# Three moves in the opening of a retention, feed-forward and expert kernel: weights through a PSUM bank, one scaling on VectorE, one output earlier

## The chip, the cores and the metric

The kernel runs on one core of a Trainium2 chip. The metric is the time of one execution in microseconds, device side; a lower time is better. TensorE is the matrix engine, VectorE (DVE), ScalarE (ACT) and GpSimd (POOL) work on vectors, and SyncE (SP) issues most transfers. Steps and chunks are counted from 0.

## The reference

Three stages in a row: retention (attention with a decay and no softmax), a feed-forward layer whose weights come in as 64-bit floats, and a layer of eight experts with a capacity of 288 tokens each.

```python
scores = scale * np.matmul(q, k.transpose(0, 1, 3, 2))          # B, H, S, D = 4, 8, 576, 64
ret = scores * np.where(rel >= 0, gamma ** rel, 0.0)
x = np.matmul(ret, v)                                            # to 2304 tokens of 512

h = x @ w_in                                                     # 512 -> 2048
g = h * np.tanh(np.log1p(np.exp(h)))
x = g @ w_out                                                    # 2048 -> 512

logits = x @ w_gate                                              # 8 experts
# the largest logits first: each token to one expert, 288 tokens to each expert
out[mask] = np.maximum(x[mask] @ w1[e], 0.0) @ w2[e]
```

## The kernel before

The change lies in `first_part`, which does the retention and the feed-forward layer; the experts follow in `second_part`, which is not touched.

The tokens go in chunks of 128 or 64 for the retention and in blocks of 256 for the feed-forward layer. A chunk has three parts. `a_scores` makes the scores on TensorE (line 223) into two PSUM banks, multiplies both by the decay on VectorE (line 228, tile `pm`), scales q on GpSimd (line 232) and k on GpSimd or VectorE (line 237). `a_out` multiplies with the running state (line 247) and with v (line 252) into a third bank, and splits the result into a high half `xh` on ScalarE (line 258) and a low half `xl` on VectorE (line 259). `a_state` adds to the state (line 277).

The feed-forward layer runs in steps: step i takes one of 16 column tiles of `w_in` and the matching tile of `w_out` for one block. `ff_h` makes `ph`, twelve products from high and low halves (line 323). `ff_a1` turns it on ScalarE into `d` (lines 332 to 334) and multiplies on VectorE (line 340, here called the product), `ff_a2` takes the reciprocal (line 345), `ff_b1` makes `u` (line 350), `ff_b2` finishes it (line 358), and `ff_b3` splits it into `gh` on ScalarE (line 364) and `gl` on VectorE or GpSimd (line 365). `ff_y` multiplies with `w_out` three steps later (line 417).

In the first 35 steps or so each step also converts a weight tile. A weight comes as 64-bit numbers of two 32-bit words. `x1` (line 163) and `c` (line 160) read them on ScalarE, `x` (line 167) and `a` (line 172) put the bits together on VectorE, `h` rounds the high half on ScalarE (line 178), and `l` takes the low half on GpSimd (line 181). Four tiles are begun ahead of step 0, so the tile whose `c` stands at the end of step i is shifted and joined in step i + 1 by

```python
        def a(self):
            t = self.t.bitcast(U32)
            nc.vector.scalar_tensor_tensor(t, t, 3, self.w0, op0=ALU.logical_shift_left,
                                           op1=ALU.bitwise_or)
```

Each engine works through its own queue in the order in which the Python code emits, and waits at the head of it. Parts of chunks 2 to 6 are put into steps by the table `EARLY` (line 30): scores of chunk 2 into step 0, its output and state into step 1, scores of chunk 3 into step 2, its output and state into step 3, scores of chunk 4 into step 4, of chunk 5 into step 5, of chunk 6 into step 7. A step that converts calls these parts behind `ff_a1` and `ff_b3`. The banks A to E go round (`bank`, line 200); from step 3 on A and B hold the output of block 0, and from step 7 on C and D that of block 1. Block 1, with steps 4 and 5, needs the outputs of chunks 2 and 3. `fill` issues products on TensorE that nobody reads (line 506).

Of the kernel before, what the change touches and what calls it, by code (L numbers as in the profile page):

```python
# [7 lines left out]
F32 = mybir.dt.float32  # L8
# [4 lines left out]
U32 = mybir.dt.uint32  # L13
U16 = mybir.dt.uint16
I64 = mybir.dt.int64
AF = mybir.ActivationFunctionType
ALU = mybir.AluOpType

P = 128
B, H, S, D = 4, 8, 576, 64  # L20
N, DM, FF, E, F = 2304, 512, 2048, 8, 1024
# [9 lines left out]
MID = (2, 3, 5, 8, 8, 9, 11, 14)  # L31
JOIN = (9, 14)
YL = 3
NF = FF // P


# [24 lines left out]
LOG2 = (3, 4, 6)  # L61
TAIL = (NB - 1) * NF


def plan():


    spread = lambda a, b, n: [a + (b - a) * k // (n - 1) for k in range(n)]
    own = {i: (0, f) for f, i in enumerate([0, 1, 2, 3] + spread(6, ENDS[0], NF - 4))}
    free = [i for i in range(3 * NF) if i not in own]  # L70
    lead = [i for i in free if i < BEGIN2]
    rest = [i for i in free if BEGIN2 <= i]
    near = [i for i in rest if i <= ENDS[1]]
    ones = lead + [near[k] for k in spread(1, len(near) - 1, NF - len(lead))]
    own.update({i: (1, f) for f, i in enumerate(ones)})
# [6 lines left out]
def first_part(ctx, tc, att, att_ht, att_hn, dtab, qtab, ktab, stab, wi, wo, wgb, ydram, L, constants, cst, begin, grid):  # L82
    nc = tc.nc
# [9 lines left out]
    D_ = big.tile([P, 2, 4, P], F32, name="dt")  # L93
# [19 lines left out]
    def load_chunk(ci):  # L113
        load_qk(ci)
        load_v(ci)
# [27 lines left out]
    class convert:  # L143
# [8 lines left out]
            self.i = done[0]  # L152
            done[0] += 1

        def c(self):
            if self.i in (2, 3):
                self.t = spare[:, self.i % 2 * 512:][:, :512]
            else:
                self.t = cvs[self.i % 2]
            nc.scalar.activation(self.t, self.w1.bitcast(F32), AF.Copy, scale=2.0 ** -112)  # L160

        def x1(self):
            nc.scalar.activation(self.w0, self.top, AF.Copy, scale=2.0 ** -13, bias=-0.4999)
# [1 line left out]
        def x(self):  # L165
            w0 = self.w0
            nc.vector.scalar_tensor_tensor(w0, self.w1, 0x80000000, w0, op0=ALU.bitwise_and,  # L167
                                           op1=ALU.bitwise_or)

        def a(self):  # L170
            t = self.t.bitcast(U32)
            nc.vector.scalar_tensor_tensor(t, t, 3, self.w0, op0=ALU.logical_shift_left,  # L172
                                           op1=ALU.bitwise_or)
            if self.i not in (6, 7):
                fetch()
# [18 lines left out]

    att_tags = ["A", "B", "C", "D", "E"]
    turn = [0]

    def bank(tag=None):  # L200
        if not tag:
            tag = att_tags[turn[0] % len(att_tags)]
            turn[0] += 1
        return psum.tile([P, 4, P], F32, tag=tag, name="b_" + tag)
# [10 lines left out]
    def a_scores(ci, halves=(0, 1), tags=(None, None), eng=nc.gpsimd):  # L215
        b, s0, n = CHUNKS[ci]
        a = at_tiles[ci]
        qT = a[:, 0, 0:4 * n].rearrange("p (h t) -> p h t", h=4)
        kT = a[:, 1, 0:4 * n].rearrange("p (h t) -> p h t", h=4)
        ts = [(s, bank(tags[s])) for s in halves]  # L220
        for hp in range(4):
            for s, t in ts:
                nc.tensor.matmul(t[:n, hp, :n], kT[s * 64:(s + 1) * 64, hp, :],  # L223
                                 qT[s * 64:(s + 1) * 64, hp, :], start=True, stop=True)
        if 0 in halves:
            pm[ci] = work.tile([P, 2, 4, P], F32, tag="pm", name="pm")
        for s, t in ts:
            nc.vector.tensor_mul(pm[ci][:n, s, :, :n], t[:n, :, :n], D_[:n, s, :, :n])
        if 1 not in halves:
            return  # L230
        if s0 > 0:
            nc.gpsimd.tensor_mul(qT, qT, Q_[:, :, :n])
        if s0 + n < S:
            kn = a[:n, 2, :].rearrange("p (h d) -> p h d", h=H)
            s1 = since(ci)
            c = 4 + (s1 + 64) // P if s1 % P or n < P else s1 // P
            eng.tensor_mul(kn, kn, K_[:n, c, :, None].to_broadcast([n, H, D]))
# [56 lines left out]
    def micro(n):  # L294

        out = []
        for ci in chunks_of(n):
            if n == 3:
                out.append([lambda ci=ci: a_scores(ci, (0,))])
                out.append([lambda ci=ci: a_scores(ci, (1,))])  # L300
            else:
                out.append([lambda ci=ci: a_scores(ci)])
            out.append([lambda ci=ci: a_out(ci)])
            out.append([lambda ci=ci: a_state(ci),
                        lambda ci=ci: load_chunk(ci + 2) if ci + 2 < len(CHUNKS) else None])
        return out
# [8 lines left out]
    def ff_h(n, f, i):  # L315
        xh, xl = x_block(n)
        if i % 2 == 0:
            hbank[0] = psum.tile([P, 2, TB], F32, tag=("ph0", "ph1")[i // 2 % 2], name="ph")
        ph = hbank[0][:, i % 2, :]
        k = 0  # L320
        for kt in range(KT):
            for w, x in ((winh, xh), (winl, xh), (winh, xl)):
                nc.tensor.matmul(ph, w[f][:, kt, :], x[:, kt, :], start=(k == 0), stop=(k == 11))  # L323
                k += 1
        q2[n, f] = ph

    def ff_a1(n, f, i, alone):

        ph = q2[n, f]
        d = work.tile([P, 2, P], F32, tag="d", name="d", bufs=2)  # L330
        df = d.rearrange("p a b -> p (a b)")
        nc.scalar.activation(df, ph, AF.Tanh, scale=0.5)  # L332
        nc.scalar.activation(df, df, AF.Square, bias=half_b, scale=-0.5)  # L333
        nc.scalar.activation(df, df, AF.Copy, bias=0.5, scale=0.5)  # L334
        u = work.tile([P, 2, P], F32, tag="u", name="u", bufs=3)
        r = u[:, 0, :]
        if alone:

            r = rs[:, i % 2 * P:][:, :P]
        nc.vector.tensor_mul(r, d[:, 0, :], d[:, 1, :])  # L340
        inv[n, f] = (d, u, r, alone)
# [144 lines left out]
    slots = {}  # L486
# [12 lines left out]
    c0, c1, old, now = [convert() for j in range(4)]  # L499
    for hp in range(WARM):  # L500
        nc.tensor.matmul(state[0][:, hp % 4, :], SD[:, 0, :], SD[:, 0, :], start=True, stop=True)
    unread = psum.tile([P, 2, TB], F32, tag="ph1", name="unread")

    def fill(n):
        for k in range(n):
            nc.tensor.matmul(unread[:, 0, :P], D_[:, 0, 0, :], D_[:, 0, 1, :], start=True, stop=True)

    a_scores(0)
    fill(2)
# [33 lines left out]
    for j, m in zip(MID, micro(3)):  # L543
        slots.setdefault(steps.index((0, NF - 1)) + YL + j, []).extend(m)
    slots.setdefault(3 * NF + 5, []).append(lambda: a_scores(chunks_of(4)[0]))
# [12 lines left out]
    for x in slots.get(-1, []):  # L558
        x()
    for i in range(len(steps) + YL):  # L560
        new = i < len(steps)
        if not i or new and not_yet(i):
            ff_h(*steps[i], i)
        if i == 20:
            constants()
        if i == 62:
            stage.__exit__(None, None, None)
            late = tc.tile_pool(name="late", bufs=1)
            WG = late.__enter__().tile([P, E, DM], F32, name="WG")
            nc.sync.dma_start(WG, wgb)  # L570
        if now:
            now.x()
            now.a()
        if old:
            old.l()
        if new:
            n, f = steps[i]
            alone = bool(now or old)
            eng = nc.vector if alone else nc.gpsimd
            if not alone:  # L580
                for x in slots.get(i, []):
                    x()
            if i and steps[i - 1] in inv:
                ff_b1(*steps[i - 1], nc.vector)
            ff_a1(n, f, i, alone)
            if i > 1:
                ff_b3(*steps[i - 2], eng)
            if alone:
                for x in slots.get(i, []):
                    x()  # L590
            if now:
                now.h()
            if alone or i == len(steps) - 2:
                ff_h(*steps[i + 1], i + 1)
            while behind:
                behind.pop()()
            ff_a2(n, f)
            if i:
                ff_b2(*steps[i - 1])
            if eng is not nc.vector:  # L600
                ff_b1(n, f, nc.vector if i == len(steps) - 1 else eng)
        if i == len(steps) - 1:
            ff_b2(n, f)
            ff_b3(*steps[i - 1], nc.gpsimd)
            ff_b3(n, f, nc.vector)
        old, now = now, None
        if nxt and i in CONV:
            now, nxt = nxt, convert() if done[0] < len(parts) else None
            now.x1()
            now.c()  # L610
        for k in range(2 if i % 4 == 0 or TAIL <= i < POP2 else 1):
            if idle:
                idle.pop(0)()
        if late and i > TAIL + BEGIN and not idle:
            late = late.__exit__(None, None, None)
            soon.extend(begin())
        if i >= YL:
            ff_y(*steps[i - YL], i)
    while idle:
# [1019 lines left out]
```

## Time and profile before

| what | us |
|---|---|
| median of three runs | 793.83 |
| lowest and highest | 793.38, 793.94 |
| the profiled execution | 800.43 |
| its span | 798.6 |
| busy: TensorE | 756.1 |
| busy: VectorE | 541.0 |
| busy: GpSimd | 483.3 |
| busy: ScalarE | 435.2 |

The span is that of one execution taken with the profiler on. It shows the order and the durations of single instructions; changes of the time are read against the median of the runs. The share of a busy engine is an average over stages that have different limits.

### The profile page before, as it was taken

The numbers are of one execution on the slowest core, as the hardware profiler recorded it, in microseconds if no ns is written. First come the engines' busy times: TensorE is split into PE (matmuls) and PEld (weight loads), VectorE is DVE, ScalarE is ACT, GpSimd is POOL, SyncE is SP. The second block draws the span as 40 slices with busy tenths as digits, with TensorE's granted clock in tenths as the row PEclk, the third lists the DMA queues.
The fourth block names the chain that finished last, engine by engine and source line by source line (L and its number), as shares of the span: only waits on it lengthen the run. The fifth ranks groups of instructions, "written<-read, shape, count | busy, mean of one in ns | idle before, by whom it ended". The sixth has DMA issues, their size and how long they took to land.

```text
span 798.6 us, 16299 instructions
## 1 busy us (share of the span) xinstructions
PE 756.1 (95%) x6163; PEld 698.4 (87%) x6163; DVE 541.0 (68%) x1260; ACT 435.2 (54%) x944; POOL 483.3 (61%) x546
## 2 busy tenths in 40 slices
PE   7799899999999999999999999949999999999995
PEld 6687777898989998989889999839899989999995
DVE  5999998555646897997988976666566754542220
ACT  4789997545445545555555564414444644644631
POOL 2643333555546676676675665327688988978921
PEclk9999999999999999999999999958999999999998
DMA  9556442010333200212010000045466567556411
GB/s 344 201 180 217 158 146 75 28 31 24 106 99 114 80 27 27 81 54 80 16 38 27 2 27 2 1 160 189 145 190 189 172 200 221 164 165 218 136 31 32
DMA packets 27380, 87.79 MB, mean 110 GB/s; under 512 B 4464, under 2 KB 5616, under 8 KB 27168
## 3 DMA queue, kind: packets, MB, share of 16 engines
q1 hardware_dynamic: 24160, 77.06, 29.7%
q0 software_dynamic: 3136, 9.64, 3.7%
q8 instruction: 49, 0.80, 0.4%
q14 instruction: 35, 0.29, 0.1%
HBM read 77.25 MB, written 9.44 MB: 109 GB/s over the span
## 4 chain that ended last, share of the span: by engine, by line
PE 72%; DVE 13%; issue 7%; POOL 2%; ACT 2%; DMA 2%; another core or an unknown queue 0%; POOLq 0%; SPq 0%; DVEq 0%; ACTq 0%
PE ph L323 20%; PE hp L1336 10%; PE op L1350 10%; PE b_E L417 8%; PE b_F L417 8%; DVE rs L345 3%; DVE y L172 2%; DVE raw L167 2%; PE cnt L1045 1%; PE b_A L223 1%; DVE u L350 1%; POOL wxl L876 1%; PE b_D L252 1%; PE b_E L453 1%; PE b_F L453 1%
## 5 line engine op out<-in xcount | busy, mean ns | idle before, releaser
L323 PE MATMUL ph<-xh,winh 128*128 128x256 f32 x576 | 164.9, 286 | 8.4 <-ACT d L332 5.4
L323 PE MATMUL ph<-xl,winh 128*128 128x256 f32 x576 | 160.7, 279 | 0.8 <-DVE xl L259 0.8
L323 PE MATMUL ph<-xh,winl 128*128 128x256 f32 x576 | 160.8, 279 | 0.0
L876 POOL TENSOR_TENSOR wxl<-wraw,wxh 128x1024 fp32r<-128x1024 f32 x63 | 149.3, 2394 | 9.0 <-ACT wxh L874 7.5
L323 PEld LDWEIGHTS ph<-xh,winh 128*128 128x128 f32 x576 | 108.5, 188 | 23.8 <-ACT d L332 9.9
L365 POOL TENSOR_TENSOR gl<-u,gh 128x256 fp32r<-128x256 f32 x114 | 88.9, 780 | 62.9 <-ACT gh L364 62.2
L332 ACT ACTIVATE d<-ph 128x256 f32<-128x256 f32 x144 | 54.9, 381 | 128.8 <-PE ph L323 114.5
L323 PEld LDWEIGHTS ph<-xh,winl 128*128 128x128 f32 x576 | 108.6, 189 | 4.0
L345 DVE RECIPROCAL u<-u 128x128 f32<-128x128 f32 x113 | 107.7, 953 | 3.9
L323 PEld LDWEIGHTS ph<-xl,winh 128*128 128x128 f32 x576 | 108.6, 189 | 1.3 <-DVE xl L259 1.3
L340 DVE TENSOR_TENSOR u<-d 128x128 f32<-128x128 f32 x113 | 53.4, 473 | 60.6 <-ACT d L334 60.0
L352 POOL TENSOR_TENSOR u<-d,u 128x128 f32<-128x128 f32 x112 | 51.7, 461 | 58.8 <-DVE u L345 58.8
L333 ACT ACTIVATE d<-d,half_b 128x256 f32<-128x256 f32 x144 | 73.5, 511 | 4.7
L874 ACT ACTIVATE wxh<-wraw 128x1024 fp32r<-128x1024 f32 x64 | 67.3, 1053 | 13.6 <-DMA wraw<-in_wx_dram 13.6
L353 POOL TENSOR_TENSOR u<-d,u 128x128 f32<-128x128 f32 x112 | 68.8, 614 | 8.8
L334 ACT ACTIVATE d<-d 128x256 f32<-128x256 f32 x144 | 60.2, 418 | 4.5
L364 ACT ACTIVATE gh<-u 128x256 fp32r<-128x256 f32 x144 | 58.1, 403 | 5.4 <-DVE u L358 4.4
L374 DVE SCALAR_TENSOR_TENSOR scr<-y,WG 128x512 bf16<-128x512 f32 x64 | 56.4, 881 | 0.4
L1327 DVE SCALAR_TENSOR_TENSOR htl<-hp,hth 128x288 fp32r<-128x288 f32 x64 | 29.1, 455 | 35.1 <-ACT hth L1339 34.2
L358 DVE SCALAR_TENSOR_TENSOR u<-u,ph 128x256 f32<-128x256 f32 x144 | 52.0, 361 | 0.0
L1339 ACT ACTIVATE hth<-hp 128x288 fp32r<-128x288 f32 x64 | 26.1, 409 | 43.4 <-PE hp L1336 34.5
L1336 PE MATMUL hp<-xth,wxh 128*128 128x288 f32 x256 | 49.4, 307 | 0.0
(299 smaller groups left out, 1874.6 us busy)
## 6 DMA issues: line engine op xcount, KB each, us to landing
wraw<-in_wx_dram SPq DMA_DIRECT2D x64, 512.0 KB, 4.4
att<-in_att_dram SPq DMA_DIRECT2D x32, 512.0 KB, 5.8
raw<-in_wi_dram SPq DMA_DIRECT2D x16, 512.0 KB
raw<-in_wo_dram SPq DMA_DIRECT2D x16, 512.0 KB, 3.2
ydram<-y SPq DMA_DIRECT2D x9, 512.0 KB, 2.8
WG<-in_wgb_dram SPq DMA_DIRECT2D x1, 2048.0 KB
att<-in_att_ht_dram SPq DMA_DIRECT2D x4, 256.0 KB
att<-in_att_hn_dram SPq DMA_DIRECT2D x4, 256.0 KB
```

The source lines that it names most:

```text
L323: nc.tensor.matmul(ph, w[f][:, kt, :], x[:, kt, :], start=(k == 0), stop=(k == 11))
L333: nc.scalar.activation(df, df, AF.Square, bias=half_b, scale=-0.5)
L334: nc.scalar.activation(df, df, AF.Copy, bias=0.5, scale=0.5)
L345: nc.vector.reciprocal(r, r)
L353: eng.tensor_mul(u[:, 0, :], d[:, 1, :], r)
L364: nc.scalar.activation(gh, g, AF.Copy)
L365: eng.tensor_sub(gl, g, gh.bitcast(F32))
L417: nc.tensor.matmul(py[n][t], g[:, t * P:(t + 1) * P], w[f], start=(f == 0 and w is woh and g is gh), stop=(f == NF - 1 and g is gl))
L874: nc.scalar.activation(hi, raw, AF.Copy)
L876: rest = lambda eng: eng.tensor_sub(lo, raw, hi.bitcast(F32))
L1336: nc.tensor.matmul(hp, W[ft // 2][w][:, s], x[:, kt, :], start=(k == 0), stop=(k == 11))
L1350: nc.tensor.matmul(op, W[4 + dt][w][:, s], h[:, ft, :], start=(k == 0), stop=(k == 23))
```

## The change

Four edits. The tiles whose `c` stands in steps 0 and 1 leave `c` in PSUM bank E, and `a` reads it there and writes the same SBUF tile as before; so that bank E is free for this, the first chunks go round four banks, and E joins them again at step 4. The k of chunk 3 is scaled on VectorE. In step 3 `ff_a1` and the parts of chunk 3 (output and state, with the loads of chunk 5) come ahead of `u` of step 2 and `gl` of step 1. Six unread products into bank E stand behind them.

```diff
+SOON = 3
...
-        def c(self):
+        def c(self, aside=False):
...
-            nc.scalar.activation(self.t, self.w1.bitcast(F32), AF.Copy, scale=2.0 ** -112)
+            self.s = bank("E").rearrange("p a b -> p (a b)") if aside else self.t
+            nc.scalar.activation(self.s, self.w1.bitcast(F32), AF.Copy, scale=2.0 ** -112)
...
-            t = self.t.bitcast(U32)
-            nc.vector.scalar_tensor_tensor(t, t, 3, self.w0, op0=ALU.logical_shift_left,
+            nc.vector.scalar_tensor_tensor(self.t.bitcast(U32), self.s.bitcast(U32), 3, self.w0, op0=ALU.logical_shift_left,
                                            op1=ALU.bitwise_or)
...
-    att_tags = ["A", "B", "C", "D", "E"]
+    att_tags = ["A", "B", "C", "D"]
...
-                out.append([lambda ci=ci: a_scores(ci)])
+                out.append([lambda ci=ci: a_scores(ci, eng=nc.vector if ci == 3 else nc.gpsimd)])
...
-    def fill(n):
+    def fill(n, to=unread[:, 0, :P]):
         for k in range(n):
-            nc.tensor.matmul(unread[:, 0, :P], D_[:, 0, 0, :], D_[:, 0, 1, :], start=True, stop=True)
+            nc.tensor.matmul(to, D_[:, 0, 0, :], D_[:, 0, 1, :], start=True, stop=True)
...
+        if i == SOON + 1:
+            att_tags.append("E")
...
-            if not alone:
-                for x in slots.get(i, []):
-                    x()
+            todo = list(slots.get(i, []))
+            if i == SOON:
+                ff_a1(n, f, i, alone)
+            if not alone or i == SOON:
+                while todo:
+                    todo.pop(0)()
             if i and steps[i - 1] in inv:
                 ff_b1(*steps[i - 1], nc.vector)
-            ff_a1(n, f, i, alone)
+            if i != SOON:
+                ff_a1(n, f, i, alone)
             if i > 1:
                 ff_b3(*steps[i - 2], eng)
-            if alone:
-                for x in slots.get(i, []):
-                    x()
+            while todo:
+                todo.pop(0)()
+            if i == SOON:
+                fill(6, bank("E")[:, 0, :])
...
-            now.c()
+            now.c(i < 2)
```

VectorE's queue from `a` of step 2 to the end of step 3, before (`y_153` holds the joined weight, `raw` its two words, `rs` the reciprocal):

```order
L172 SCALAR_TENSOR_TENSOR y_153<-y_153,raw 128x512
L350 TENSOR_TENSOR u<-d,rs 128x256
L340 TENSOR_TENSOR rs<-d 128x128
L365 TENSOR_TENSOR gl<-u,gh 128x256
L228 TENSOR_TENSOR pm<-b_E,dt 128x512
L228 TENSOR_TENSOR pm<-b_A,dt 128x512
L345 RECIPROCAL rs<-rs 128x128
...
L350 TENSOR_TENSOR u<-d,rs 128x256
L340 TENSOR_TENSOR rs<-d 128x128
L365 TENSOR_TENSOR gl<-u,gh 128x256
L259 TENSOR_TENSOR xl<-b_B,xh 128x4x128
```

The same stretch of VectorE's queue after (lines are one to two numbers higher):

```order
L173 SCALAR_TENSOR_TENSOR y_153<-b_E,raw 128x512
L351 TENSOR_TENSOR u<-d,rs 128x256
L341 TENSOR_TENSOR rs<-d 128x128
L366 TENSOR_TENSOR gl<-u,gh 128x256
L229 TENSOR_TENSOR pm<-b_B,dt 128x512
L229 TENSOR_TENSOR pm<-b_C,dt 128x512
L238 TENSOR_TENSOR att<-att,kt 128x512
L346 RECIPROCAL rs<-rs 128x128
...
L341 TENSOR_TENSOR rs<-d 128x128
L260 TENSOR_TENSOR xl<-b_D,xh 128x4x128
L351 TENSOR_TENSOR u<-d,rs 128x256
L366 TENSOR_TENSOR gl<-u,gh 128x256
```

The first operation reads bank E and not `y_153`; the k of chunk 3 (`att<-att,kt`) has come in ahead of the reciprocal; and in step 3 the product and `xl` have moved ahead of `u` and `gl`.

TensorE's queue at the end of step 3, before:

```order
L247 MATMUL b_B<-att,sd 128x128 x4
L252 MATMUL b_B<-pm,att 64x128 x8
L277 MATMUL b_F<-att 64x64 x8
L323 MATMUL ph<-xh,winh_76 128x256
L323 MATMUL ph<-xh,winl_92 128x256
L323 MATMUL ph<-xl,winh_76 128x256
```

And after:

```order
L248 MATMUL b_D<-att,sd 128x128 x4
L253 MATMUL b_D<-pm,att 64x128 x8
L278 MATMUL b_F<-att 64x64 x8
L507 MATMUL b_E<-dt 128x128 x6
L324 MATMUL ph<-xh,winh_76 128x256
L324 MATMUL ph<-xh,winl_92 128x256
L324 MATMUL ph<-xl,winh_76 128x256
```

The six unread products stand between the state of chunk 3 and the first `ph` of block 1; the output of chunk 3 is in another bank. On GpSimd the k of chunk 3 is gone; all else stands in the same order, and the transfers on SyncE do too.

## Rows read from the trace of the kernel before

**Rows 1.** Windows: stretch in us, its length, each engine's busy us (instructions), granted clock, DMA.

```profile
60.00:131.00 71.00, 64.51 (x411) 52.91 (x410) 69.01 (x147) 67.26 (x147) 25.94 (x21) 1.00 0.50 167
131.00:798.60 667.60, 641.77 (x5255) 601.87 (x5254) 422.60 (x1030) 327.06 (x710) 430.00 (x501) 0.98 0.29 92
```

**Rows 2.** Timeline of VectorE, steps 1 to 3: start us, us, line, what [idle before].

```profile
25.05 1.58 DVE L172 SCALAR_TENSOR_TENSOR y<-y,raw 128x512 uint32<-128x512 uint32 x1
...
29.73 1.61 DVE L172 SCALAR_TENSOR_TENSOR y<-y,raw 128x512 uint32<-128x512 uint32 x1
31.27 1.26 DVE L350 TENSOR_TENSOR u<-d,rs 128x256 f32<-128x256 f32 x1
32.45 1.35 DVE L340 TENSOR_TENSOR rs<-d 128x128 f32<-128x128 f32 x1
...
34.66 0.68 DVE L228 TENSOR_TENSOR pm<-b_A,dt 128x512 f32<-128x512 f32 x1
...
38.66 0.68 DVE L259 TENSOR_TENSOR xl<-b_B,xh 128x512 fp32r<-128x512 f32 x1
```

**Rows 3.** Timeline of GpSimd, steps 1 to 4.

```profile
24.36 1.73 POOL L181 TENSOR_TENSOR winl<-spare,winh 128x512 fp32r<-128x512 f32 x1
...
28.94 1.85 POOL L232 TENSOR_TENSOR att<-att,qt 128x512 f32<-128x512 f32 x1 [0.28 <-POOL wol L181]
30.74 1.51 POOL L237 TENSOR_TENSOR att<-att,kt 128x512 f32<-128x512 f32 x1
32.21 1.45 POOL L181 TENSOR_TENSOR wol<-y,woh 128x512 fp32r<-128x512 f32 x1
38.61 1.28 POOL L181 TENSOR_TENSOR wol<-y,woh 128x512 fp32r<-128x512 f32 x1 [4.96 <-ACT woh L178]
42.97 0.75 POOL L232 TENSOR_TENSOR att<-att,qt 128x256 f32<-128x256 f32 x1 [3.08 <-issue]
```

**Rows 4.** Timeline of TensorE: unread products, then step 3 and the first of block 1.

```profile
12.70 0.94 PE L506 MATMUL unread<-dt 128*128 128x128 f32 x6
...
34.80 0.43 PE L252 MATMUL b_B<-pm,att 128*64 128x128 f32 x2 [2.46 <-DVE pm L228]
...
39.40 0.39 PE L323 MATMUL ph<-xl,winh 128*128 128x256 f32 x1 [0.46 <-DVE xl L259]
```

**Rows 5.** Timeline of ScalarE: `c` at the end of step 1.

```profile
28.77 0.70 ACT L160 ACTIVATE y<-raw 128x512 f32<-128x512 f32 x1
```

**Rows 6.** Windows of TensorE's wait in step 3 and the stretch behind it.

```profile
32.30:34.80 2.50, 0.04 (x2) 0.01 (x1) 2.50 (x5) 2.02 (x5) 1.36 (x1) 1.00 0.63 210
34.80:37.40 2.60, 2.43 (x25) 2.19 (x27) 2.50 (x5) 0.42 (x1) 0.00 (x0) 0.61 0.00 0
```

**Rows 7.** Timeline of VectorE, step 5 and steps 7 to 8.

```profile
45.63 1.35 DVE L172 SCALAR_TENSOR_TENSOR y<-y,raw 128x512 uint32<-128x512 uint32 x1
...
54.41 0.69 DVE L172 SCALAR_TENSOR_TENSOR y<-y,raw 128x512 uint32<-128x512 uint32 x1
...
55.56 0.42 DVE L365 TENSOR_TENSOR gl<-u,gh 128x256 fp32r<-128x256 f32 x1
55.91 0.69 DVE L228 TENSOR_TENSOR pm<-b_C,dt 128x512 f32<-128x512 f32 x1
...
59.04 1.60 DVE L172 SCALAR_TENSOR_TENSOR y<-y,raw 128x512 uint32<-128x512 uint32 x1
```

**Rows 8.** Timeline of GpSimd, step 7.

```profile
56.05 1.32 POOL L232 TENSOR_TENSOR att<-att,qt 128x512 f32<-128x512 f32 x1 [2.50 <-PE b_D L223]
57.32 1.05 POOL L237 TENSOR_TENSOR att<-att,kt 128x512 f32<-128x512 f32 x1
58.32 1.76 POOL L181 TENSOR_TENSOR wol<-y,woh 128x512 fp32r<-128x512 f32 x1
```

**Rows 9.** Timeline of TensorE, step 7: the first of twelve `ph`, and L417.

```profile
55.81 0.38 PE L323 MATMUL ph<-xh,winh 128*128 128x256 f32 x1
...
57.33 0.40 PE L417 MATMUL b_C<-woh,gh 128*128 128x512 f32 x1
```

## The prediction

> **What bounds the kernel now.** I read the windows first, then the timelines of the opening engine by engine, and last the places where VectorE and GpSimd run side by side. Between 60 and 131 us VectorE is busy 69.01 of 71 us while TensorE is busy 64.51; from 131 us on TensorE is busy 641.77 of 667.60 us [rows 1]. So VectorE paces the opening, in which weights are still converted, and TensorE the rest. What the opening loses or gains on VectorE's line reaches the end; a gain on TensorE's line alone does not, since it then waits for VectorE.
>
> In the opening VectorE loses time in one way: an operation whose two inputs both lie in SBUF stands still while a GpSimd operation runs. L172 takes 0.69 us alone [rows 7], but 1.58 at 25.05 and 1.61 at 29.73 [rows 2]. The GpSimd operation of 24.36 ends at 26.09 and that of 28.94 at 30.79 [rows 3]; the two L172 end 0.54 and 0.55 us behind these. The u of 31.27 (1.26) and the product of 32.45 (1.35) end 0.28 and 0.14 behind the GpSimd operations of 30.74 and 32.21 [rows 2, 3]. GpSimd waits too: its 128x512 subtraction takes 1.28 alone at 38.61, but 1.73 at 24.36 [rows 3]. Operations that read one operand from PSUM are not touched: L228 of step 7 (55.91) runs in 0.69 next to the GpSimd operation of 56.05 [rows 7, 8]. I count steps and chunks from 0, so the fourth of each is number 3.
>
> The Trainium skill (SBUF — State Buffer, Who interferes with whom) states this as a rule: a VectorE instruction with two SBUF inputs and a GpSimd instruction that reads SBUF hold a shared port in turn, for the whole instruction. These rows agree with it (ends 0.14 to 0.55 us behind the other's end). By that rule the k that is moved to VectorE would contend too, which speaks against that part; in the sum below it meets only the last 0.1 us of a GpSimd operation.
>
> **The change part by part.**
>
> *PSUM input for L172, steps 1 and 2.* The first ends at 25.74 and not 26.63. The u behind it still has two SBUF inputs and waits until 26.09, so 0.6 of the 0.89 stays. In step 2, L172 can then start at 29.2 and end at 29.9, not at 31.34: 1.4. What c costs when ScalarE writes PSUM no row shows. The nearest is the same operation into SBUF, 0.70 at 28.77 [rows 5]; it ends 0.2 us before L172 needs it, so anything up to 0.9 is free, and at twice its price step 2 starts 0.5 later. I take 0.70. L172 with a PSUM operand I take at 0.69: L228, the row nearest to it, has that width, one PSUM operand and 0.69 [rows 7].
>
> *k on VectorE.* GpSimd loses the operation of 30.74 (1.51, of which 0.5 was waiting) [rows 3]. VectorE gains one of that width, 0.69 as for L228 and L172 alone [rows 7], of which 0.6 is added to its line, since starts overlap. With L172 out of the way, u waits only for GpSimd's q (28.8 to 30.3) and ends at 30.6; the product of 32.45 runs unblocked at 30.5, and the second L228 starts at 31.6, not 34.66: 3.0 earlier. With k behind it, 2.4 are left on VectorE's line, and two blocked operations are gone.
>
> *Output ahead of u and gl, step 3.* u and gl (0.42 alone, 0.34 from start to start) go behind xl: 0.7. xl starts at 35.7, not 38.66, and TensorE's first product that reads it at 36.4, not 39.40: TensorE is 3.0 ahead. Its wait of 2.46 before 34.80 [rows 4], after which the granted clock was 0.61 [rows 6], nearly vanishes.
>
> *Six unread products.* Six records of three such products took 0.94 [rows 4], so six products about 1.6 at most, from 33.7 to 35.3. They lie under TensorE's wait for xl and cost nothing; were xl there at once, they would cost that 1.6. They write bank E, whose last reader ended at 29.9.
>
> *What is late next.* (1) GpSimd's low half of a weight in step 3 (38.61) hangs on L172 of that step by way of ScalarE, so it moves with VectorE's line by 2.3, to 36.3, where u and gl now stand: one of them waits, about 1.1. VectorE is then 1.2 ahead, TensorE still 3.0. (2) GpSimd's q for chunk 4 follows TensorE: 42.97 becomes 40.0, just where L172 of step 4 starts; if GpSimd is first, L172 loses 0.6. Before, L172 of step 5 lost 0.66 at 45.63 [rows 7]; with GpSimd's work there moved ahead by more than VectorE's, it no longer does. VectorE stays about 1.3 ahead. (3) Step 7 decides. There GpSimd has q, k and the low half of a weight in a row, 56.05 to 60.08 [rows 8], and now they fall under L228, L228 and the reciprocal: q starts when VectorE is past gl of 55.56, and only L172 of 59.04 waits, 0.91 [rows 7]. q follows TensorE, which nothing holds up between xl and there, so it moves to 53.0; VectorE's L172 of that step moves only from 54.41 to 53.1. q then meets L172, k meets u, the low half meets the product: the pattern of 29.73 to 33.80, whose price was 0.92 + 0.84 + 1.07 = 2.8 (each row of [rows 2] less 0.69, 0.42 and an estimated 0.28 for half of that width). I take 3.0, since q itself starts just ahead of L172. VectorE goes from 1.3 ahead to 1.7 behind, and gains back the 0.91 at 59.04: 0.8 behind. (4) Now L228 of chunk 6 starts at 57.6. TensorE has finished the ph ahead of L417 at 54.2 (57.33 less 3.1), and L417 writes bank C [rows 9], which L228 reads: it idles some 4 us until 58.3. In the 2.6 us behind the idle 2.46 the granted clock was 0.61, mostly the lower level of 1.2 GHz [rows 4, 6]. The twelve ph took 1.52 (55.81 to 57.33); the six L417 are twice as wide and half as many, so as much again, and at 1.2 GHz the two take about 2.5 more. VectorE's xl of step 9 hangs on them through the output of chunk 6. TensorE's slack is 6.49 us over 21 steps in [rows 1] (147 VectorE instructions, seven a step), 0.3 a step: of 2.5, two steps hide 0.6, and 1.9 arrive.
>
> Sum at the end of the opening: -1.3 + 3.0 - 0.9 + 1.9 = **+2.7 us**. Behind step 10 VectorE paces alone and gives nothing back. The profiled execution, 800.43 with a span of 798.6, would become 803.1; it lies 6.6 above the median of the runs, and I assume the opening to run alike in both: 793.83 + 2.7 = 796.5.
>
> **Rivals.** *The gain is kept* (faster). One mechanism: at step 7 q stays out of the way of L172, u and the product. It decides where q starts relative to L172 of that step: 0.1 us ahead by my sum, 1.64 behind it before. If q is 1.4 or more behind, only gl or L228 stand beside it. That needs TensorE to arrive 1.5 us later than I say, as it would if its clock falls in step 3 in spite of the unread products, for which the fall of the clock after the wait of 2.46 speaks [rows 4, 6]. Then 1.3 is left, or 2.2 if the 0.91 at 59.04 goes as well: 791.6 to 792.5; I take 792.1. Against it: 1.5 us is more than any single term that I left open.
>
> *The ports only.* The three waits at step 7 come, but TensorE idles less than it must for the clock to fall, or its slack hides the slow products: +0.8, 794.6. The wait of 2.46 with its 0.61 speaks against it.
>
> *The tie at step 4 falls to VectorE.* q of chunk 4 and L172 come within 0.05 us. If L172 is first, q, a low half and k stand against u, the product and gl, 1.1 behind instead of 0.8 ahead; since TensorE then waits too, some 1.6 of it reaches the end: +4.3, 798.1. The page named above says that of the two, the one that issues first holds the port; by that rule either order is open here, and the time would be this rival's or the forecast's.
>
> *The change does not do what it says.* The waits that leave step 2 are paid one for one elsewhere, without the clock: 793.8, give or take 0.5.
>
> **How the numbers follow.** Forecast 0.43, its own range 795.6 to 797.3; gain kept 0.30; ports only 0.14; tie 0.08; nothing 0.05. Faster by over 0.2% (1.6 us, about what a measurement of this kernel can tell from no change) takes two thirds of "gain kept": 0.20. Within 0.2%: the rest of it, "ports only" and "nothing": 0.29. Slower: forecast and tie, 0.51. The range goes from 791.8 (a third of "gain kept" left out) to 798.1 (half of the tie left out), 8 in 10.
>
> **What would show it.** Right: L172 at 0.69 in steps 1 and 2; the second L228 near 31.6; xl near 35.7; L172, u and product of step 7 at 1.3 to 1.7 us each, from 53 us on; TensorE idle 4 us before L417 near 58 with a granted clock below 1 behind it; the reciprocals behind step 10 some 2.7 later. Wrong: GpSimd's q of chunk 6 starting behind gl again, TensorE without that wait, and the reciprocals earlier than before. If c into PSUM takes over 0.9, or L172 is still at 1.6 with a PSUM operand, the first step of the sum falls.

## The result: 5 us slower, and the profile after

| | us |
|---|---|
| before, median of four runs | 793.88 (793.38 to 794.13) |
| after, median of four runs | 799.01 (798.64 to 800.21) |
| ratio, with its 95% interval | 1.0062 (1.0048 to 1.0076) |
| forecast, and its range | 796.5 (791.8 to 798.1) |

The time lies 0.9 us outside the range, and the loss is 5.1 us where 2.7 were forecast. A ratio comes with an interval of its own and is not exactly the quotient of the two medians, which is 1.0065 here; where the two differ much, both are given. The two profiled executions, 800.43 and 800.21 us with spans of 798.6 and 798.4, seem to say that nothing has changed. They have to be read by stretch: the reciprocal of step 20 starts at 103.53 us before and at 108.68 after, 5.15 later; this lead of the old kernel stands until 476 us (481.49 against 476.46) and melts away only among the experts, where that one execution of before lost some 6 us that the median of its runs doesn't have. So the whole loss arises in the opening. The lead or lag of VectorE there, step by step, is the start of the reciprocal (L345 before, L346 after) less that of before; a minus is a lead. Each row is one profiled execution, and step 0, ahead of what the change does, already differs by up to 0.4. It reads, in us, with the experiments below:

| step | 0 | 3 | 4 | 5 | 7 | 8 | 10 | 20 |
|---|---|---|---|---|---|---|---|---|
| after | 0.0 | -1.2 | +1.0 | +0.2 | +3.2 | +2.3 | +4.8 | +5.2 |
| nudge | -0.3 | -1.6 | -1.2 | -1.7 | +1.3 | +0.4 | +2.1 | +2.1 |
| late_q4 | -0.1 | -1.4 | -1.6 | -1.7 | -1.8 | -1.8 | -1.7 | -1.2 |
| late_q6 | -0.1 | -1.4 | +0.9 | +0.1 | +0.6 | +0.6 | +0.6 | +1.2 |
| keep_busy | 0.0 | -1.2 | +1.0 | +0.2 | +3.3 | +2.3 | +2.6 | +2.9 |
| no_reorder | -0.2 | -2.6 | -1.1 | -1.0 | -1.1 | -1.1 | -1.1 | -0.7 |
| no_reorder_fill | 0.0 | -2.4 | -2.4 | -2.4 | -2.4 | -2.4 | -2.4 | -1.6 |
| no_reorder_fill2 | 0.0 | -2.4 | -2.4 | -2.3 | -2.4 | -2.4 | -2.3 | -1.9 |
| k6_too | -0.2 | -2.6 | -2.6 | -2.6 | -1.9 | -2.8 | -2.5 | -2.3 |
| reorder_alone | -0.2 | +0.9 | +1.2 | +0.8 | +1.9 | +1.0 | +1.2 | +1.2 |
| no_fill | 0.0 | -1.3 | +0.9 | +0.1 | +3.2 | +2.2 | +5.0 | +5.4 |
| early_q4 | -0.4 | -2.7 | +0.9 | +0.1 | +3.1 | +2.2 | +3.8 | +3.8 |
| after_again | -0.4 | -1.7 | +0.6 | -0.2 | +2.8 | +1.9 | +3.7 | +4.1 |

Steps 1 to 3 do what they were meant to. VectorE's timeline of after, against [rows 2] (start, us, line, what):

```profile
25.09 0.69 DVE L173 SCALAR_TENSOR_TENSOR y<-b_E,raw 128x512 uint32<-128x512 uint32 x1
25.69 0.71 DVE L351 TENSOR_TENSOR u<-d,rs 128x256 f32<-128x256 f32 x1
...
29.26 0.69 DVE L173 SCALAR_TENSOR_TENSOR y<-b_E,raw 128x512 uint32<-128x512 uint32 x1
...
31.66 0.67 DVE L229 TENSOR_TENSOR pm<-b_C,dt 128x512 f32<-128x512 f32 x1
32.26 0.73 DVE L238 TENSOR_TENSOR att<-att,kt 128x512 f32<-128x512 f32 x1
...
35.65 0.68 DVE L260 TENSOR_TENSOR xl<-b_D,xh 128x512 fp32r<-128x512 f32 x1
36.25 0.41 DVE L351 TENSOR_TENSOR u<-d,rs 128x256 f32<-128x256 f32 x1
36.58 1.52 DVE L366 TENSOR_TENSOR gl<-u,gh 128x256 fp32r<-128x256 f32 x1
```

L173 takes 0.69 with its operand in PSUM where it took 1.58 and 1.61; xl starts 3.0 earlier. Step 4 is where it turns. VectorE and GpSimd there, from their timelines:

```profile
39.95 0.69 DVE L173 SCALAR_TENSOR_TENSOR y<-y,raw 128x512 uint32<-128x512 uint32 x1
40.56 0.96 DVE L351 TENSOR_TENSOR u<-d,rs 128x256 f32<-128x256 f32 x1
41.44 1.40 DVE L341 TENSOR_TENSOR rs<-d 128x128 f32<-128x128 f32 x1
42.76 1.26 DVE L366 TENSOR_TENSOR gl<-u,gh 128x256 fp32r<-128x256 f32 x1
```

```profile
40.01 1.23 POOL L233 TENSOR_TENSOR att<-att,qt 128x256 f32<-128x256 f32 x1 [2.18 <-issue]
41.38 1.30 POOL L182 TENSOR_TENSOR winl<-y,winh 128x512 fp32r<-128x512 f32 x1
42.65 1.08 POOL L238 TENSOR_TENSOR att<-att,kt 64x512 f32<-64x512 f32 x1
```

L173 has come 0.06 us ahead of q. q (0.75 alone) waits for it, and u, the product and gl then wait for q, the low half and k, one each: 0.55, 1.11 and 0.84 above what they take alone. The same pattern stands in step 7, with 0.05 us between L173 and q:

```profile
54.64 0.69 DVE L173 SCALAR_TENSOR_TENSOR y<-y,raw 128x512 uint32<-128x512 uint32 x1
55.25 1.51 DVE L351 TENSOR_TENSOR u<-d,rs 128x256 f32<-128x256 f32 x1
56.69 1.12 DVE L341 TENSOR_TENSOR rs<-d 128x128 f32<-128x128 f32 x1
57.73 1.48 DVE L366 TENSOR_TENSOR gl<-u,gh 128x256 fp32r<-128x256 f32 x1
```

```profile
54.69 1.79 POOL L233 TENSOR_TENSOR att<-att,qt 128x512 f32<-128x512 f32 x1 [1.06 <-PE b_D L224]
56.44 1.23 POOL L238 TENSOR_TENSOR att<-att,kt 128x512 f32<-128x512 f32 x1
57.63 1.31 POOL L182 TENSOR_TENSOR wol<-y,woh 128x512 fp32r<-128x512 f32 x1
```

In step 7 the order does not set the price. In `after_again` (the changed kernel once more) q came first, at 54.20 against 54.22, so that L173, u and the product waited, and VectorE lost 3.0 there too. VectorE's timeline of after_again, then GpSimd's q:

```profile
54.22 1.82 DVE L173 SCALAR_TENSOR_TENSOR y<-y,raw 128x512 uint32<-128x512 uint32 x1
55.96 1.26 DVE L351 TENSOR_TENSOR u<-d,rs 128x256 f32<-128x256 f32 x1
57.14 1.36 DVE L341 TENSOR_TENSOR rs<-d 128x128 f32<-128x128 f32 x1
```

```profile
54.20 1.29 POOL L233 TENSOR_TENSOR att<-att,qt 128x512 f32<-128x512 f32 x1 [1.00 <-PE b_D L224]
```

In after, TensorE then has nothing to do until VectorE has read bank C, and comes back at a granted clock of 0.50, which is the lower level, 1.2 GHz. TensorE's timeline of after, then windows of the same places (stretch, length, busy us of PE, PEld, DVE, ACT and POOL, granted clock, DMA), then the xl of step 9 that waits for it:

```profile
55.84 0.28 PE L324 MATMUL ph<-xl,winh 128*128 128x256 f32 x1
59.88 0.79 PE L418 MATMUL b_C<-woh,gh 128*128 128x512 f32 x1 [3.75 <-DVE pm L229]
60.47 0.63 PE L418 MATMUL b_C<-wol,gh 128*128 128x512 f32 x1
```

```profile
56.10:59.90 3.80, 0.05 (x2) 0.03 (x1) 3.80 (x5) 3.23 (x9) 2.84 (x3) 0.80 0.88 302
59.90:63.50 3.60, 3.60 (x11) 3.02 (x12) 3.50 (x8) 0.93 (x2) 0.00 (x0) 0.50 0.32 118
```

```profile
69.33 0.69 DVE L260 TENSOR_TENSOR xl<-b_E,xh 128x512 fp32r<-128x512 f32 x1 [1.81 <-ACT xh L259]
```

So the loss of 5.15 is 0.2 up to step 5, 3.0 in step 7, -0.9 in step 8, 2.5 in steps 9 and 10, and 0.36 in step 16.

### The profile page after: what moved, and what is told of

Its sections match the earlier page's. It is cut to its first block, busy times and chain, and to the rows that moved or that the text cites. A ratio compares the mean times of both kernels' runs of the same rounds, so it can differ in the third digit from the quotient of the medians.

```text
span 798.4 us, 16325 instructions
## 1 busy us (share of the span) xinstructions
PE 759.4 (95%) x6175; PEld 701.3 (88%) x6175; DVE 543.5 (68%) x1261; ACT 435.3 (55%) x944; POOL 482.1 (60%) x545
## 4 chain that ended last, share of the span: by engine, by line
PE 73%; DVE 11%; issue 7%; POOL 3%; ACT 2%; DMA 2%; POOLq 0%; SPq 0%; DVEq 0%; ACTq 0%
PE ph L324 21%; PE hp L1344 11%; PE op L1358 10%; PE b_E L418 8%; PE b_F L418 8%; DVE rs L346 3%; DVE raw L169 2%; PE cnt L1053 1%; DVE y L173 1%; POOL wxl L884 1%; PE b_A L224 1%; DVE u L351 1%; PE b_F L454 1%; PE b_E L454 1%; PE b_D L253 1%
## 5 line engine op out<-in xcount | busy, mean ns | idle before, releaser
L346 DVE RECIPROCAL u<-u 128x128 f32<-128x128 f32 x113 | 107.7, 953 | 3.9
```

What stands on the lines that cost most here:

```text
L346: nc.vector.reciprocal(r, r)
```

## Experiments

The theory (A): the time is set by when TensorE reaches the scores of chunks 4 and 6, because q follows them onto GpSimd and then stands beside VectorE's operations with two inputs in SBUF; a late VectorE starves TensorE, and its clock falls. The rivals: the moved work itself costs (B); the lag is the same whenever q comes. Ratios are to before on the same chip. Where unread products or a clearing are added, nobody reads what they write.

### Later q of chunk 4, later q of chunk 6

`late_q4`:

```diff
+            if i == 4:
+                fill(6, bank("E")[:, 0, :])
             while todo:
```

> The changed kernel with six more unread products in step 4, ahead of the scores of chunk 4, 1.4 to 1.6 us of TensorE: q of chunk 4 starts near 41.5 and not at 40.01, behind u and the product of step 4 instead of beside them. Theory A (the order in which q and VectorE's operations arrive decides, and a later q of chunk 4 also brings a later q of chunk 6): the waits of 0.54, 1.12 and 0.84 at step 4 shrink to about 0.5 together, step 4 is some 2.5 earlier, TensorE's lead is mostly gone by step 7, the waits there and the idle time of TensorE vanish, and the time is 792.7 to 793.6. Theory B (the moved work costs) and the theory that step 7 pays whatever step 4 does: 796 or more.

793.37 us, ratio 0.9989 (0.9979 to 0.9999): 5 to 6 us less than the changed kernel, for 1.4 us more work on TensorE. q starts at 41.17, u, the product and gl of step 4 take 0.42, 0.28 and 0.42, and nothing is left of the waits of step 7 or of TensorE's. These products delay TensorE as a whole, so by itself this run does not part step 4 from step 7.

`late_q6`, the same at `i == 7` with `fill(8, ...)`:

> The changed kernel with eight more unread products in step 7, ahead of the scores of chunk 6, 1.8 us of TensorE: q of chunk 6 starts near 56.5 and not at 54.69, when u and the product of step 7 are through or nearly; step 4 is untouched and stays 1.0 behind. Theory A: of the three waits at step 7 (1.09, 0.84, 1.06) at most one is left, TensorE does not idle 3.75 us before L418, its clock stays at 1.00, and the time is 794.3 to 795.6, 3.5 to 4.7 less than the changed kernel. Rival (the time of q does not matter, GpSimd's three operations cost VectorE the same wherever they fall): 798 or more.

794.93 us, ratio 1.0009 (0.9999 to 1.0020). q of chunk 6 starts at 56.63, behind gl (55.63); step 7 costs 0.5 (a wait of 0.44 for the scores) and not 3.0, and the clock term is gone with it. L173 of step 8 waits its 0.9 again. Both say A; the rival that the lag doesn't depend on q's time falls.

### The tie of step 4

`nudge`:

```diff
+        if i == SOON + 1:
+            nc.vector.memset(bank("E")[:, 0, :], 0.0)
         if now:
             now.x()
```

> The changed kernel with one more piece of work: VectorE clears 128x128 of bank E ahead of L169 in step 4 (0.17 us for such a clearing elsewhere in the trace of before; nobody reads it). L173 of step 4 then starts 0.1 to 0.2 later than 39.95, and q of chunk 4, at 40.01, is first. Theory A (step 4 was lost by a tie of 0.06 us): L173 waits once, about 0.6, u, the product and gl no longer wait 3 times, the reciprocal of step 4 starts 1.4 to 2.0 us earlier than in the changed kernel, TensorE keeps its lead, step 7 still takes 3 us and the clock 2: in all 3.0 to 4.0 above before, 1.2 to 2.0 below the changed kernel, by doing 0.2 us more. Rival (what VectorE loses at step 4 is the same in either order): 0 to 0.3 above the changed kernel.

797.04 us, ratio 1.0041 (1.0026 to 1.0055), and the unchanged `after_again` on the same chip 798.88: by the medians 1.84 less, by doing more. VectorE's timeline of nudge, and GpSimd's:

```profile
38.92 0.17 DVE L575 MEMSET b_E<- 128x128 f32 x1
39.00 0.67 DVE L169 SCALAR_TENSOR_TENSOR raw<-raw 128x512 uint32<-128x512 uint32 x1
39.77 1.13 DVE L173 SCALAR_TENSOR_TENSOR y<-y,raw 128x512 uint32<-128x512 uint32 x1
40.82 0.42 DVE L351 TENSOR_TENSOR u<-d,rs 128x256 f32<-128x256 f32 x1
41.16 0.28 DVE L341 TENSOR_TENSOR rs<-d 128x128 f32<-128x128 f32 x1
41.36 0.41 DVE L366 TENSOR_TENSOR gl<-u,gh 128x256 fp32r<-128x256 f32 x1
```

```profile
39.61 0.74 POOL L233 TENSOR_TENSOR att<-att,qt 128x256 f32<-128x256 f32 x1 [2.14 <-issue]
41.65 1.30 POOL L182 TENSOR_TENSOR winl<-y,winh 128x512 fp32r<-128x512 f32 x1 [1.29 <-ACT winh L179]
```

q is first and L173 alone waits, 0.44. GpSimd's low half then waits for ScalarE's high half until 41.65, and u, the product and gl pass ahead of it. From here on nudge is the scenario of the forecast, and VectorE's -1.7 in step 5 and +2.1 in step 20 answer to the forecast's -1.3 and +2.7; by the ratio the time is 3.3 above before. The Trainium skill (SBUF — State Buffer, Who interferes with whom) says of this in one sentence, "Issue order, not op shape, decides who blocks." The two traces agree: L173 did not wait in after, where it came 0.06 us ahead of q, and waited 0.44 in nudge, where it came 0.16 behind.

> The changed kernel as it is, beside the others on the same chip: 4.5 to 5.5 us above before, if the opening runs as in its first profile.

Ratio 1.0056 (1.0041 to 1.0071), so 4.4 us, or 5.2 by the medians.

`early_q4` puts the scores of chunk 4 at the end of step 3:

```diff
-EARLY = (0, 1, 1, 2, 3, 3, 4, 5, 5, 5, 6, 7, 7, 9, 9)
+EARLY = (0, 1, 1, 2, 3, 3, -5, 5, 5, 5, 6, 7, 7, 9, 9)
...
+        for x in (slots.get(-5, []) if i == SOON else []):
+            x()
         if i >= YL:
```

> The changed kernel with the scores of chunk 4 put at the end of step 3, ahead of the L418 there, so that its q runs near 38.5, beside the reciprocal, and not at 40.01 beside u and the product of step 4. TensorE keeps its lead of 3.0 us. Theory A (two separate places: step 4 turns on a tie, step 7 on TensorE's lead): step 4 is no later than before (-0.5 to 0), q of chunk 6 falls on L173, u and the product of step 7 all the same, 3 us there, TensorE idles over 3 us, and the time is 2.8 to 4.0 above before, 1.2 to 2.2 below the changed kernel. Rival (step 7 pays only because step 4 was late): at or below before.

805.3 us, ratio 1.0057 (1.0037 to 1.0077), 4.6 us above before and not 2.8 to 4.0. The expectation missed at step 4. q ran at 38.24, but it took 1.81 beside VectorE's operations, and GpSimd's low half that runs at 36.27 in after now stood behind it (40.01) and met u; step 4 was +0.9 again. Step 7 cost 3.0 and TensorE waited 3.75 us, but since step 4 was late once more, this run can't settle whether step 7 pays only because of that. nudge settles it: there VectorE is 1.7 ahead in step 5, and step 7 costs 3.0 as well.

### The clock

`keep_busy`:

```diff
                 ff_h(*steps[i + 1], i + 1)
+            if i == 7:
+                fill(15, bank("E")[:, 0, :])
             while behind:
```

> The changed kernel with 15 more unread products in step 7, behind the twelve ph and ahead of L418, where TensorE idled 3.75 us (55.96 to 59.88): at 0.227 us each they fill 3.4 of it. The three waits of VectorE on GpSimd at step 7 stay. Theory A (of the 5.1 us lost, 2.2 to 2.5 come from the lower clock behind this idle time): L418 takes 0.40 and not 0.63, xl of step 9 waits 0 to 0.4 and not 1.81, and 1.9 to 2.5 are gained against the changed kernel: 796.5 to 797.2. Rival (it is TensorE's late start, not its clock, that makes xl late): 799.0 as the changed kernel.

797.16 us, ratio 1.0035 (1.0022 to 1.0048), 1.9 us less than after by the medians. Windows of keep_busy at the places shown above for after, and L418:

```profile
56.10:59.90 3.80, 3.37 (x32) 3.18 (x30) 3.80 (x5) 3.27 (x9) 2.87 (x3) 1.00 0.92 255
59.90:63.50 3.60, 3.60 (x21) 3.04 (x22) 3.50 (x8) 0.91 (x2) 0.00 (x0) 1.00 0.44 167
```

```profile
59.90 0.50 PE L418 MATMUL b_C<-woh,gh 128*128 128x512 f32 x1 [0.43 <-DVE pm L229]
60.24 0.39 PE L418 MATMUL b_C<-wol,gh 128*128 128x512 f32 x1
```

L418 starts no earlier than in after (59.90 and 59.88), yet xl of step 9 no longer waits and step 10 is 2.2 us earlier. So those 2.2 us are the clock's, not the late start's; the other 0.3 of steps 9 and 10 are still there.

### Without the reorder

`no_reorder` takes back edits three and four:

```diff
-            if i == SOON:
+            if False:
                 ff_a1(n, f, i, alone)
-            if not alone or i == SOON:
+            if not alone:
...
-            if i != SOON:
+            if True:
                 ff_a1(n, f, i, alone)
...
-                fill(6, bank("E")[:, 0, :])
+                pass
```

> The changed kernel without its third and fourth edit: in step 3 the product and the output of chunk 3 stand behind u and gl again, and the six unread products are gone; c through PSUM and k of chunk 3 on VectorE stay. Theory A (the loss hangs on when q of chunks 4 and 6 starts on GpSimd, and it is the early output that moves q): xl of chunk 3 goes back to about 36.4, TensorE is then 2.2 ahead of before and VectorE 2.3, the two stay in step, q of chunk 6 starts behind gl of step 7 as before, and 1.2 to 2.3 us are gained against before: 791.6 to 792.7. Theory B (the price is that of the moved work itself: the scaling that VectorE has gained and the c in PSUM): slower than before still, 795 or more. Theory C (bank E missing from the round, or the early output is where the gain is): about 793.9 or above.

793.35 us, ratio 0.9984 (0.9969 to 0.9999), 1.3 us less than before by the ratio, at the low end of what A gives. B and C fall, C by little: PSUM input and the k on VectorE win 2.4 us between steps 0 and 3. But 1.5 of it goes in step 4. TensorE and VectorE of no_reorder (windows first):

```profile
33.80:36.80 3.00, 0.51 (x2) 0.30 (x2) 2.90 (x8) 2.39 (x7) 0.78 (x1) 1.00 0.57 168
36.80:40.00 3.20, 3.19 (x15) 2.81 (x16) 2.79 (x6) 2.71 (x7) 0.50 (x1) 0.66 0.05 12
```

```profile
39.92 0.29 DVE L341 TENSOR_TENSOR rs<-d 128x128 f32<-128x128 f32 x1 [0.31 <-ACT d L335]
...
41.79 0.42 DVE L229 TENSOR_TENSOR pm<-b_C,dt 64x256 f32<-64x256 f32 x1 [1.14 <-PE b_D L224]
```

TensorE was nearly idle for 3 us, its clock fell, and now VectorE waits for it. `no_reorder_fill` is the same kernel with `fill(10, bank("E")[:, 0, :])` where after has six:

> Without the reorder, as no_reorder, but with ten unread products in step 3, behind the state of chunk 3 (2.3 us of TensorE, 33.7 to 36.0), where TensorE idled 1.18 and 1.43 us in no_reorder and its granted clock then fell to 0.50 (38 to 40 us). Theory A (no_reorder has kept only 1.1 of the 2.6 us that VectorE was ahead after step 3, because the slow TensorE brought the scores of chunk 4 late, VectorE idle 1.14 and 0.31 there): the clock stays at 1.00, the scores of chunk 4 come before VectorE wants them, and 2.0 to 2.5 us are gained against before instead of 1.0. Rival (q of chunk 4, now earlier, meets VectorE's line at step 4): no more than the 1.0 of no_reorder.

798.85 us on a chip where before takes 800.65, ratio 0.9980 (0.9963 to 0.9996). The windows of no_reorder_fill there:

```profile
33.80:36.80 3.00, 2.73 (x24) 2.53 (x22) 2.90 (x7) 2.21 (x7) 0.60 (x1) 1.00 0.39 126
36.80:40.00 3.20, 3.02 (x25) 2.50 (x27) 3.04 (x7) 2.96 (x8) 0.67 (x1) 1.00 0.24 56
```

The 2.4 us of step 3 are kept to step 10, but only 1.6 to step 20, and the time is 1.6 less by the ratio, not the 2.0 to 2.5 expected. Once more, beside after_again:

> no_reorder_fill once more, on the chip of the changed kernel: the opening 1.6 to 2.4 us ahead of before, 1.5 to 2.3 less in time, and 6 to 7.5 less than the changed kernel.

792.2 us, ratio 0.9977 (0.9965 to 0.9988), 1.8 us less than before by the ratio and 6.7 less than after_again, as expected. `k6_too` adds the k of chunk 6 to it (`eng=nc.vector if ci in (3, 6) else nc.gpsimd`):

> no_reorder_fill with the k of chunk 6 on VectorE as well, in step 7. VectorE gains about 0.6 us there; GpSimd's low half of step 7 starts 1.0 earlier, so that L173 of step 8 no longer waits 0.9 for it. Theory A: 0.2 to 0.4 us less than no_reorder_fill. Rival (the wait only moves to another operation with two SBUF inputs): 0.3 to 0.6 more than no_reorder_fill.

791.09 us, ratio 0.9964 (0.9950 to 0.9977), 2.6 us less than before by the medians on that chip, and the best here. Of the two expectations A's holds in the profile: -2.4 in step 8 becomes -2.8, or 0.2 counted from step 0. The 1.1 us by the medians is more than A gives; 0.36 of it is a wait in step 16 that is missing here (see below), which the edit was not made for. That it beats no_reorder_fill2 is likely and not certain, since the intervals overlap.

### The reorder alone, and the six products taken away

`reorder_alone` keeps edits three and four, and takes back the first two:

```diff
-                out.append([lambda ci=ci: a_scores(ci, eng=nc.vector if ci == 3 else nc.gpsimd)])
+                out.append([lambda ci=ci: a_scores(ci, eng=nc.gpsimd)])
...
-            now.c(i < 2)
+            now.c()
```

> The third and fourth edit alone: the output of chunk 3 ahead of u and gl in step 3, with six unread products; c in SBUF and k of chunk 3 on GpSimd as before (the round of banks is still that of the changed kernel). Theory A (the early output is what costs, since TensorE comes early to the scores of chunks 4 and 6): slower than before by 4.5 to 6.5 us, with the three waits at step 7 and TensorE idle over 3 us behind them. Theory B (only all edits together cost): within 1 us of before.

803.03 us, ratio 1.0046 (1.0022 to 1.0071): slower, as A says, but by the ratio 3.7 us (2.4 by the medians) and not 4.5 to 6.5. The profiled execution, 799.33, is the fastest of its twelve and lost only 1.2 in the opening, without A's three waits in step 7 and its long wait of TensorE (0.88 us there): TensorE waited 2.48 us for pm ahead of 34.60, the granted clock from 34.6 to 38.0 was 0.52, and q of chunk 6 came late enough (56.20) to miss u and the product. What the other runs, up to 808.8 us, did there no trace shows.

`no_fill` only has `pass` in place of the six products:

> The changed kernel without its six unread products in step 3, its other three edits kept. TensorE then idles about 2 us in two pieces before it can use xl of chunk 3 (33.9 to 36.4). Theory A with a fallen clock, as in no_reorder after waits of 1.18 and 1.43: the twelve ph and six L418 of step 3 take 1.3 to 1.5 us longer, q of chunk 4 starts behind u and the product of step 4, no waits there and at step 7, and the time is 1.0 to 1.7 us below before. If the clock does not fall: as the changed kernel, 4.8 to 5.4 above before.

800.96 us, ratio 1.0017 (0.9992 to 1.0042), undecided against before: its runs spread from 798.5 to 807.2 us. In the profiled one (803.58) TensorE waited 0.34 and 1.63 us ahead of xl, the clock stayed at 1.00, and the opening ran as in after. The case with a fallen clock, which I had expected, would fit the runs near 798.5, but I have no trace of one.

## Why the prediction was wrong

**What bounds, and how VectorE loses.** Right that all that was lost or won arrived on VectorE's line, and that an operation with two inputs in SBUF stands still beside GpSimd. But not all of it came in that way: 2.2 us came as a wait of xl for a slow TensorE, as step (4) of the prediction itself has it, and 0.36 in a way that stays open.

**Steps 1 to 3.** Right to 0.1 us: L173 at 0.69, c into PSUM 0.65 (0.70 taken), the second L229 at 31.66 (31.6), xl at 35.65 (35.7), gl's wait in step 3 1.1 (1.1), VectorE 1.2 ahead and TensorE 3.0.

**Step (2), q of chunk 4.** This is the step that failed. I saw that q and L172 of step 4 would meet "just where L172 of step 4 starts", priced the case with GpSimd first (0.6) and took it; the other order stood as a rival with 0.08. VectorE was first, in every profile of a kernel that kept this place (by 0.02 to 0.07 us). That is 1.0 behind in step 4, where the rival's sentence gives the forecast 0.8 ahead (its own terms, 1.2 less 0.6, give 0.6), and 0.2 behind in step 5, where the forecast has 1.3 ahead: in step 5 0.8 came back, since L173 no longer waited. The rival had the lag right (1.1) and a price of 1.6; nudge shows 1.84 us of time. It ended at 798.1, 0.9 too low, so the tie alone does not make the miss: of the 2.45 us between +2.7 and +5.15, 1.5 came here, 0.6 with the clock and 0.36 in step 16. Two starts whose forecast differs by less than the error of their sum are not a case of 0.08; the two orders should have had about the same chance, and the range should have held both in full.

**Step (3), step 7.** The sum was right: 3.0 forecast, 3.0 measured, and 0.9 back in step 8. Its cause had shifted. q was to come at 53.0 because TensorE ran on; it came at 54.69, since TensorE had waited for VectorE in step 4. VectorE was later by as much (54.64 and not 53.1), so they met again, and u, the product and gl paid instead of L172, u and the product. That the sum came out all the same was luck: the sum did not look at the other order, which happens to cost as much, as after and after_again show. The three waits follow from TensorE being ahead and from three GpSimd operations in a row, and late_q6, whose only edit delays the scores of chunk 6, takes them away.

**Step (4), the clock.** The mechanism was right, and the size within what executions differ by: 1.9 forecast for steps 9 and 10, 2.5 in after and 2.8 in no_fill, 1.7, 1.8 and 1.7 in nudge, after_again and early_q4. keep_busy, which only fills the wait, gives 2.2 of the 2.5 back.

**The six unread products** cost nothing in the profiled executions, as forecast: in after TensorE waits another 0.67 us for xl behind them. I took them to keep TensorE's clock up in step 3; no_fill doesn't confirm that, for its clock held in the profiled execution too. By the ratios no_fill (1.0017) lies below after (1.0062) and after_again (1.0056), though on another chip, so over all executions the products may cost more than they give. That is not shown: the execution of no_fill that was profiled (803.58) lies above the median of its runs.

**The rest, 0.4.** L173 of step 16 waits 0.46 us in after, 0.36 more than its usual gap, with nothing in its way that I could find: the profile names ScalarE's d, but what L173 needs of ScalarE had ended 1.3 us before. The same 0.46 stands at step 16 in eight other runs, at step 29 in nudge (133.78) and early_q4 (135.50), and nowhere in the opening of before, reorder_alone or k6_too. The number of VectorE operations ahead does not settle where it falls, since up to step 16 early_q4 has as many as after. In each of the eleven traces that have it, a transfer of 8 KB in the queue that the profile lists as "q14 instruction" starts 0.66 to 0.94 us behind that L173. So it may have to do with the loading of instructions, but no run tests that, and the cause stays open.

## What to carry to other kernels

When one engine gets ahead in a stage, look at what it triggers on the others: here 3 us won on TensorE moved GpSimd's scalings under VectorE's operations with two SBUF inputs, and a gain of 2.4 became a loss of 5. Where two such operations are forecast to start within a few tenths of a microsecond, work out both orders and give both a real chance; the price of an order also hangs on what the other engine has ready next (the orders are 1.8 us apart at step 4, and equal at step 7). And where a change is made of parts, time it without each part: two of the four edits here, with some unread products to keep TensorE's clock up, beat both kernels.

## What I had not expected

A clearing of 0.17 us on VectorE made the kernel 1.84 us faster, and 1.4 us of products that nobody reads made it 5 us faster. From waits of a few microseconds I could not have forecast TensorE's granted clock: behind waits of 1.18 and 1.43 us it was 0.66 (no_reorder, 36.8 to 40.0), behind one of 2.48 us 0.52 (reorder_alone), behind waits of 0.34 and 1.63 us 1.00 (no_fill), and behind one of 3.75 us 0.50 (after).
